# Four start-up memsets moved from GpSimd to VectorE, matmuls on ones ahead of the first transposes, and the order of 2,902 jobs read from a table

## The chip, the cores and the metric

The kernel runs on one core of one Trainium2 chip. A core has five engines with instruction streams of their own: TensorE (PE; PEld is its weight load), VectorE (DVE), ScalarE (ACT), GpSimd (POOL) and SyncE (SP). They meet through semaphores. SP and POOL issue the DMAs here, and sixteen DMA engines move the data. The metric is device time in microseconds.

## The reference

Linformer attention in 8 batches with 8 heads, 1024 tokens and head size 64, followed by a gated feed-forward layer on the 8192 tokens:

```python
k_proj = np.einsum('ks,bhsd->bhkd', E, k)            # 1024 keys become 64
v_proj = np.einsum('ks,bhsd->bhkd', F, v)
scores = scale * np.matmul(q, k_proj.transpose(0, 1, 3, 2))
scores = scores - np.max(scores, axis=-1, keepdims=True)
attn = np.exp(scores)
attn = attn / (np.sum(attn, axis=-1, keepdims=True) + 1e-09)
x = np.matmul(attn, v_proj)                          # as (8192, 512)
gate = 1.0 / (1.0 + np.exp(-(x @ w_gate)))           # w_gate, w_val: (512, 1536)
val = x @ w_val
out = gate * val @ w_out                             # w_out: (1536, 512)
```

Inputs and output are float32; the matmuls run in bfloat16.

## The kernel before

**Tiling.** A batch is cut into two blocks of 512 tokens. For each batch the kernel projects keys and values by E and F, transposes the queries (by DMA through SP from batch 1 on), computes scores, subtracts the row maximum, takes the exponential, multiplies by the projected values and transposes the quotient into `xT`. The gated layer of a block then reads `xT`. Most of its products are done as seven smaller products instead of eight (`seven`, `o_jobs`), so VectorE and GpSimd add and subtract operands and partial results; the first block and parts of the last go the plain way (`plain_steps`, `o_plain`). Eight PSUM banks (`pF0` to `pF3`, `pA0` to `pA3`) and thirteen float32 buffers of 512 columns hold what is in flight; two of the buffers lie in `EF`.

**The start.** `start_loads` issues E and F on SP (L629). On POOL it first sets the four 32-partition pieces of `quad` to 0, 32, 64 and 96 (L635) and then issues 25 loads (L569) in this order: keys, first query half and again for the other four heads, values, quarters of the gate and value weights, with the second query halves between them. `constants` builds identity matrices on VectorE: a row of counts by doubling (L660), its first 32 columns transposed (L667), `quad` added (L669), and comparisons into `identf`, `ident` and `minus` (L675, L682). It then clears `kpd` (L689) and two `vpD` (L693), and writes columns of ones (L696). `project_consts` turns E and F by eight float32 transposes on TensorE (L528) into two banks, and ACT copies both to `EFT` (L542).

**What sets the order.** Everything after that is a *job*: a Python function that issues one or more instructions on one engine, with a position given by the tables `AT` and `FB`. A `Scheduler` plays the program forward with costs, release times (`K_AT`, `Q_AT`, `V_AT`, `LAND`) and due positions. Whenever an engine of its model is free it takes the first job that is ready and for which a bank or buffer is free, so it decides the order on each engine and the place of each bank and buffer. When TensorE has nothing to do before its 25th microsecond it places a filler: two matmuls of 128 columns on `ident` into bank 7, which nobody reads. `Plan` adds the semaphore waits that follow from the resulting order, and each engine runs its list strictly in that order.

**Names in the trace.** Nearly all matmuls have L528, all ACT copies and functions L542, plain sums of two operands L557 on VectorE or GpSimd, loads L569. On VectorE L914 copies projected keys, L989 sums exponentials, L1645 takes the maximum, L1672 subtracts it, L886 copies out of PSUM, L1066 multiplies gate and value. Stores of a row block are L1312, of half a row block L1370, both on SP.

```python
            load_part(1, v, 0)
            for th in range(2):
                load_part(1, v, 1, th)
            load_w(0, 0)
            load_w(0, 1)
            load_w(3)
            load_w(1)
            for R in range(2):
                load_q_half(0, 1, R)
            load_w(4)
            load_w(2)
            load_w(5)
```

Of the kernel before, what the change touches and what calls it, by code (L numbers as in the profile page):

```python
# [12 lines left out]
P = 128  # L13
S = 1024
DH = 64
# [138 lines left out]
class Job:  # L154
    def __init__(self, eng, pos, body, release, name):
        self.eng, self.pos, self.body, self.release, self.name = eng, round(pos, 6), body, release, name
        self.cost, self.bytes, self.dma, self.port = 0.0, 0, False, False
        self.deps, self.slots, self.start, self.end = {}, [], None, None


class Scheduler:

    TAIL = {"PE": 0.0, "ACT": 0.115, "DVE": 0.09, "POOL": 0.15, "SP": 0.0}
    HOP = {"PE": 0.205, "ACT": 0.035, "DVE": 0.035, "POOL": 0.06, "SP": 0.1}

    EXTRA = dict(
        qt=0.12, qt1=0.16, turnk=0.1, turnk0=0.1, tp=0.1, tx=0.1, tk=0.1, tq=0.1, bc0=0.8, den0=0.2, xo0=0.2,
        copyG=0.028, copyV=0.028, copyO=0.028, tanh=0.015, kd=0.1, vd=0.1,
    )

    def __init__(self, banks, bufs, t0, window, landed, busy0, warm):
        self.jobs, self.now, self.t0, self.window, self.landed = [], None, t0, window, landed
        self.busy0, self.warm, self.fillers = busy0, warm, []
        self.writers, self.readers = {}, {}
        self.free = {
            "bank": {b: t0 for b in banks},
            "buf": {b: t0 for b in bufs},
        }
        self.clean = {b: False for b in banks}
        self.groups = []  # L180
        self.reads = []
        self.more = {"ACT": AT["pact"], "DVE": AT["pdve"], "POOL": AT["ppool"]}

    def job(self, eng, pos, body, release=0.0, name=""):
        j = Job(eng, pos, body, release, name)
        self.jobs.append(j)
        self.now = j
        body()
        j.cost += self.EXTRA.get(name, 0.0)
        self.now = None  # L190
        return j

    def note(self, eng, r, w, x, dma, cost, nbytes, port):
        j = self.now
        j.port = j.port or port
        assert eng == j.eng, (eng, j.eng, j.name)
        j.cost += cost
        j.bytes += nbytes
        j.dma = j.dma or dma is not None

        def dep(o, raw):
            if o is not j:
                j.deps[o] = j.deps.get(o, False) or raw

        for k in tuple(r) + tuple(w) + tuple(x):
            if isinstance(k, tuple) and isinstance(k[1], Slot) and k[1] not in j.slots:
                j.slots.append(k[1])
                k[1].left += 1
        for k in r:
            if k in self.writers:  # L210
                dep(self.writers[k], True)
        for k in tuple(w) + tuple(x):
            if k in self.writers:
                dep(self.writers[k], False)
            for o in self.readers.get(k, ()):
                dep(o, False)
        for k in r:
            self.readers.setdefault(k, []).append(j)
        for k in tuple(w) + tuple(x):
            self.writers[k] = j  # L220
            self.readers[k] = []

    def seen(self, o, eng, raw):
        if o.dma:
            return o.end + 0.1
        if o.eng == eng:
            if eng == "PE":
                return o.start + o.cost
            return o.end + 0.02
        if o.eng in ("ACT", "DVE", "POOL") and eng == "PE":  # L230
            return o.end + 0.055
        return o.end + self.HOP[o.eng]

    def safe(self, group, got):
        left = {k: len(f) for k, f in self.free.items()}
        left["clean"] = sum(self.clean[b] for b in self.free["bank"])
        for g, b in got:
            left[g.kind] -= 1
            if g.kind == "bank":
                left["clean"] -= self.clean[b]  # L240
        taken = [g for g, _ in got]
        todo = []
        for g in self.groups + ([] if any(group is x for x in self.groups) else [group]):
            need, held = dict.fromkeys(left, 0), dict.fromkeys(left, 0)
            for x in g:
                if x.at is None and not any(x is y for y in taken):
                    need[x.kind] += 1
                    need["clean"] += x.clean
                elif x.left:
                    held[x.kind] += 1  # L250
                    held["clean"] += x.kind == "bank" and not x.dirty
            todo.append((need, held))
        while todo:
            for i, (need, held) in enumerate(todo):
                if all(need[k] <= left[k] for k in left):
                    for k in left:
                        left[k] += held[k]
                    del todo[i]
                    break
            else:  # L260
                return False
        return True

    def take(self, j, t):
        got = []
        for s in j.slots:
            if s.at is not None:
                continue
            taken = [b for g, b in got if g.kind == s.kind]
            mine = [b for b, a in self.free[s.kind].items() if a <= t and b not in taken]  # L270
            if s.kind == "bank":
                if s.clean:
                    mine = [b for b in mine if self.clean[b]]
                elif s.dirty:
                    rough = sum(not c for c in self.clean.values()) + sum(self.clean[b] for _, b in got)
                    mine = [b for b in mine if not self.clean[b] or rough < (7 if t < 25.0 else 3)]
                mine.sort(key=lambda b: (self.clean[b], self.free["bank"][b]))
            else:
                mine.sort(key=lambda b: self.free["buf"][b])
            if not mine:  # L280
                return False
            got.append((s, mine[0]))
        if not got:
            return True
        group = got[0][0].group
        if not self.safe(group, got):
            return False
        if not any(group is g for g in self.groups):
            self.groups.append(group)
        for s, b in got:  # L290
            s.at = b
            del self.free[s.kind][b]
            if s.dirty:
                self.clean[b] = False
        return True

    def running(self, j):
        return any(x.group is g for x in j.slots for g in self.groups)

    def place(self, j, t):  # L300
        j.start = t
        j.cost *= 1 + self.more.get(j.eng, 0.0)
        if j.port:
            if j.eng == "DVE":
                j.cost += max(0.0, self.held - t)
                self.lock = t + j.cost
            if j.eng == "POOL":
                j.cost += max(0.0, self.lock - t)
                self.held = t + j.cost
        j.end = t + j.cost + self.TAIL[j.eng]  # L310
        if j.dma:
            begin = max(self.pipe, t + j.cost + 1.3)
            self.pipe = begin + j.bytes / 390e3
            j.end = self.pipe + 0.9 + AT["pdma"]
        self.busy[j.eng] = t + j.cost
        for s in j.slots:
            s.left -= 1
            s.end = max(s.end, j.end + (0.25 if j.eng == "PE" else 0.055))
            if s.left == 0:
                self.free[s.kind][s.at] = s.end  # L320
                if s.kind == "bank" and not s.clean:
                    self.clean[s.at] = not s.dirty
                if all(x.at is not None and not x.left for x in s.group):
                    self.groups = [g for g in self.groups if g is not s.group]
        for k in self.after.get(j, ()):
            self.count[k] -= 1
            if self.count[k] == 0:
                ready = max([self.seen(o, k.eng, raw) for o, raw in k.deps.items()] + [k.release, self.t0])
                self.open[k.eng].append((k.pos, self.rank[k], ready, k))

    def run(self):
        engines = ("PE", "ACT", "DVE", "POOL", "SP")
        self.busy = dict(self.busy0)
# [4 lines left out]
        for j in self.jobs:  # L338
            self.count[j] = len(j.deps)
            for o in j.deps:  # L340
                self.after.setdefault(o, []).append(j)
# [1573 lines left out]
```

## Time and profile before

| what | value |
|---|---|
| time, median of 3 runs | 518.52 us (518.36 to 518.65) |
| profiled execution | span 517.0 us; its time outside the span is not recorded, the median is 1.5 us above the span |
| chain of work that ended last | PE 93%, DVE 5%, DMA 1% |
| TensorE's first matmul | at 5.49 us, when F has landed |
| stores, issue to landing | 2.3 us (median of 63) |
| DMA engines, mean | 138 GB/s over the span |
| HBM | 60.29 MB read, 16.78 MB written |

One row of a view "instructions in order of time" has the start, the length, the engine, the line, the operation and the tile it writes and reads; equal neighbours are merged (x12), and the bracket gives the idle time before and what ended it. A matmul row's length contains the pipeline, so the distance between starts tells the pace. The granted clock in the views is 1.00 everywhere.

### The profile page before, as it was taken

How to read it: one execution, taken by the hardware profiler on the slowest of the kernel's cores; microseconds unless marked ns; L12 is line 12 of the kernel's file. 1: busy time of each engine (PE TensorE's matmuls, PEld its weight loads, DVE VectorE, ACT ScalarE, POOL GpSimd, SP SyncE). 2: the span in 40 equal slices, each digit the busy share in tenths (PEclk: the TensorE clock that was granted, in tenths of full speed). 3: DMA queues.
4: the chain of work that ended last, by engine and by line, in shares of the span. 5: the costliest groups of instructions: out<-in, count | busy, mean ns of one | idle time of the engine just before them, and what ended most of it. 6: DMA issues, size and time to landing. Idle time of an engine off the chain costs nothing.

```text
span 517.0 us, 12313 instructions
## 1 busy us (share of the span) xinstructions
PE 508.4 (98%) x4786; PEld 428.2 (83%) x4786; DVE 444.8 (86%) x843; ACT 375.4 (73%) x715; POOL 171.6 (33%) x200
## 2 busy tenths in 40 slices
PE   5999999999999999999999999999999999999997
PEld 4655867889988898888988889888998889888885
DVE  5879998898999799996999969997999969999570
ACT  1566966879977697777967689776877779677752
POOL 9882004802353024430344313630244303403200
DMA  9999928796689636994489926997369963610204
GB/s 160 198 198 207 202 64 161 117 215 136 123 174 203 161 58 129 187 185 132 82 160 170 191 76 95 188 204 146 77 113 183 202 143 62 145 42 1 82 1 164
DMA packets 140522, 71.59 MB, mean 138 GB/s; under 512 B 97200, under 2 KB 132272, under 8 KB 140464
## 3 DMA queue, kind: packets, MB, share of 16 engines
q0 software_dynamic: 35904, 29.89, 37.4%
q1 hardware_dynamic: 104560, 40.91, 36.9%
q8 instruction: 38, 0.62, 0.5%
q14 instruction: 20, 0.16, 0.1%
HBM read 60.29 MB, written 16.78 MB: 149 GB/s over the span
## 4 chain that ended last, share of the span: by engine, by line
PE 93%; DVE 5%; DMA 1%; ACT 0%; issue 0%; POOL 0%; SPq 0%
PE pA L528 47%; PE pF L528 46%; DVE topf L1645 1%; DVE hT L1066 1%; DMA EF<-in_F_dram 1%; DVE pA L1672 1%; DVE pF L1672 1%; DVE inv L989 0%; ACT KVs L542 0%; POOL wT L996 0%; DVE tG L557 0%; ACT ost L542 0%; DVE inv L990 0%; DVE eT L886 0%; DVE xT L886 0%
## 5 line engine op out<-in xcount | busy, mean ns | idle before, releaser
L542 ACT ACTIVATE spare<-pF 128x512 f32<-128x512 f32 (+2 forms) x167 | 93.7, 572 | 30.5 <-PE pF L528 27.6
L557 POOL TENSOR_TENSOR hT<-hT,hS 128x512 bf16<-128x512 bf16 x42 | 48.6, 1184 | 193.7 <-PE pA L528 155.1
L542 ACT ACTIVATE spare<-pA 128x512 f32<-128x512 f32 (+2 forms) x150 | 85.1, 582 | 15.6 <-PE pA L528 12.0
L542 ACT ACTIVATE spare<-spare 128x512 f32<-128x512 f32 x77 | 48.5, 635 | 25.7 <-DVE spare L1156 25.4
L1734 POOL TENSOR_TENSOR KVs<-spare,inv 128x384 bf16<-128x384 f32 (+1 forms) x50 | 36.6, 738 | 86.9 <-ACT spare L542 43.6
L528 PE MATMUL pA<-wO,hT 128*128 128x256 bf16 (+1 forms) x408 | 60.7, 288 | 0.0
L1225 DVE SCALAR_TENSOR_TENSOR hT<-spare,pF 128x512 bf16<-128x512 f32 x73 | 48.9, 679 | 7.6 <-ACT spare L542 3.6
L528 PEld LDWEIGHTS pA<-wO,hT 128*128 128x128 bf16 x408 | 39.9, 98 | 10.4
L1156 DVE TENSOR_TENSOR spare<-pF,spare 128x512 f32<-128x512 f32 x62 | 41.8, 681 | 3.7 <-PE pF L528 2.0
L528 PE MATMUL pF<-xT,wV 128*128 128x256 bf16 (+1 forms) x276 | 44.7, 283 | 0.0
L528 PE MATMUL pF<-xS,tV 128*128 128x256 bf16 x248 | 37.3, 273 | 0.0
L1156 DVE TENSOR_TENSOR spare<-pA,spare 128x512 f32<-128x512 f32 x53 | 35.7, 676 | 1.3 <-ACT spare L542 0.8
L528 PE MATMUL pA<-xT,wG 128*128 128x256 bf16 (+1 forms) x212 | 34.1, 283 | 0.0
L528 PE MATMUL pF<-xS,wV 128*128 128x256 bf16 x224 | 33.6, 272 | 0.2 <-ACT KVs L542 0.2
L1225 DVE SCALAR_TENSOR_TENSOR hT<-spare,pA 128x512 bf16<-128x512 f32 x41 | 27.7, 679 | 5.8 <-PE pA L528 3.8
L528 PE MATMUL pF<-xT,wG 128*128 128x256 bf16 (+1 forms) x196 | 32.4, 288 | 0.2 <-DVE xT L886 0.2
L528 PEld LDWEIGHTS pF<-xT,wV 128*128 128x128 bf16 x276 | 26.6, 98 | 5.9 <-issue 0.2
L528 PE MATMUL pA<-wT,hT 128*128 128x256 bf16 x240 | 31.1, 272 | 0.0
L1672 DVE TENSOR_TENSOR pF<-pF,topf 128x512 f32<-128x512 f32 x45 | 29.7, 689 | 0.0
L1645 DVE TENSOR_REDUCE topf<-pF 128x8 f32<-128x512 f32 x45 | 29.3, 678 | 0.0
L528 PE MATMUL pF<-wO,hT 128*128 128x256 bf16 (+1 forms) x204 | 29.3, 285 | 0.0
L528 PE MATMUL pA<-wT,hS 128*128 128x256 bf16 x216 | 29.1, 273 | 0.0
(183 smaller groups left out, 1267.0 us busy)
## 6 DMA issues: line engine op xcount, KB each, us to landing
out_dram<-ost SPq DMA_DIRECT2D x63, 256.0 KB, 2.3
KVs<-in_v_dram POOLq DMA_DIRECT2D x15, 512.0 KB, 11.2
KVs<-in_k_dram POOLq DMA_DIRECT2D x14, 512.0 KB, 7.6
Qb<-in_q_dram POOLq DMA_DIRECT2D x14, 512.0 KB, 15.7
wO<-in_moe_w_out_dram POOLq DMA_DIRECT2D x1, 1536.0 KB, 28.5
wG<-in_moe_w_gate_dram POOLq DMA_DIRECT2D x5, 256.0 KB, 16.8
wV<-in_moe_w_val_dram POOLq DMA_DIRECT2D x5, 256.0 KB, 17.5
KVs<-in_k_dram POOLq DMA_DIRECT2D x4, 256.0 KB, 6.8
```

The lines of the kernel that those rows point to most:

```text
L528: lambda e: e.matmul(o, lhsT, rhs, **kw),
L542: lambda e: e.activation(o, i, func, scale=scale),
L557: fn = lambda e: e.tensor_tensor(o, a, b, op)
L1066: lambda e: e.scalar_tensor_tensor(hT[0][:, m, :], BF(sg), 1.0, PB(bv)[:, :], ALU.add, ALU.mult),
L1156: lambda e: e.tensor_tensor(PB(b)[:, :] if stay else BF(s), PB(b)[:, :], BF(s), ALU.add),
L1225: lambda e: e.scalar_tensor_tensor(o, y.rearrange("p (j c) -> p j c", j=2), 1.0, x.rearrange("p (j c) -> p j c", j=2), ALU.add, ALU.mult,),
L1645: lambda e: e.tensor_reduce((top if by_pe(b, t, y) else topf)[:, n : n + 8], PB(bk)[:, :].rearrange("p (n k) -> p n k", n=8), mybir.AxisLi ...
L1672: lambda e: e.tensor_tensor(x, x, topf[:, n : n + 8].unsqueeze(2).to_broadcast([P, 8, 64]), ALU.subtract),
L1734: fn = lambda e: e.tensor_tensor(xto.rearrange("p (g h d) -> p h g d", g=2, h=H)[:, hh[0] : hh[1], :, :], o[:, :, 0:DH].rearrange("p (h g) ...
```

## The change

- The four memsets of `quad` move from POOL, where they stood ahead of the first load, to VectorE, behind the transposition of the counts.
- VectorE first sets a new tile `warm` (128 x 128, bfloat16) to one. Ten matmuls of 512 columns on it, into bank 7, stand on TensorE ahead of the transposes of E and F.
- Of the two copies to `EFT`, ACT does the first and VectorE the second.
- The two memsets of `vpD` are written as float32, 520 columns instead of 1040.
- A filler is one matmul of 256 columns instead of two of 128. There are 35 of them instead of 45 pairs (90).
- The `Scheduler` keeps no costs any more. A table `ORDER` gives the order of all jobs (-1 is a filler), a table `PLACES` the bank or buffer of each. The 2,902 jobs, their engines and what they compute are those of before. Of the jobs on TensorE 868 of 1,054 stand at another place in its list, by up to 30 places; on VectorE 646 of 814, by up to 32; on ACT 524 of 712, POOL 109 of 167 and SP 94 of 155.

In POOL's list a load of keys of batch 1 comes ahead of eight sums of weights and of the two query loads of batch 1; before it stood behind them. In SP's list the last stores come in another order: the store of the last block's first row block stands behind that of the first half row block, and the last one is the same. On TensorE the matmuls after the last filler are the same, in another order.

The two tables, cut to their first lines, and the rest of the diff without the removed scheduler:

```diff
+ORDER = (
+    0, -1, -1, -1, 1, 2, 3, -1, -1, -1, -1, -1, -1, 12, 4, 13, 14, 5, -1, -1, 6, 15, 16, 22, 17, -1, -1, 7, 23,
...
+    def run(self, fill):
+        groups = []
         for j in self.jobs:
...
+            self.now = j
+            j.body()
+            for s in j.slots:
+                if not any(s.group is g for g in groups[-40:]):
+                    groups.append(s.group)
+        self.now = None
+        slots = [s for g in groups for s in g]
+        assert len(ORDER) - ORDER.count(-1) == len(self.jobs) and len(PLACES) == len(slots)
+        for s, p in zip(slots, PLACES):
+            s.at = p
+        return [fill if i < 0 else self.jobs[i].body for i in ORDER]
...
-            for i in range(4):
-                pool(
-                    lambda e, i=i: e.memset(quad[32 * i : 32 * i + 32, :], 32.0 * i),
-                    w=[("quad", i)],
                 )
...
         def constants():
+            dve(lambda e: e.memset(warm[:, :], 1.0), [], ["warm"])
             dve(lambda e: e.memset(count[:, 0:1], 0.0), [], ["count"])
...
             dve(lambda e: e.transpose(rows[:, :], pats[:, :]), ["pats"], ["rows"])
+            for i in range(4):
+                dve(lambda e, i=i: e.memset(quad[32 * i : 32 * i + 32, :], 32.0 * i), [], [("quad", i)], n=1)
...
-                dve(lambda e, i=i: e.memset(vpD[i][:, :, :, :], 0.0), [], vk, n=520)
+                dve(
+                    lambda e, i=i: e.memset(
+                        vpF[i][:, :].bitcast(FP32), 0.0
+                    ),
...
+        def warm_up():
+            for _ in range(10):
+                mm(7, bank[7][:, :], warm[:, :], warm[:, :].unsqueeze(1).to_broadcast([P, 4, P]), ["warm"])
...
-                act(
-                    EFT[:, 4 * g : 4 * g + 4, :].rearrange("p t c -> p (t c)"),
-                    bank[b][:, :],
-                    [],
-                    [("EFT", g)],
-                    b=b,
-                )
-
-        def busy(n):
-            for _ in range(n):
-                mm(7, bank[7][:, 0:P], ident[:, :], ident[:, :], ["ident"], n=P)
+                o = EFT[:, 4 * g : 4 * g + 4, :].rearrange("p t c -> p (t c)")
+                if g:
+                    dve(lambda e, o=o, b=b: e.tensor_copy(o, bank[b][:, :]), [], [("EFT", g)], b=b)
+                else:
+                    act(o, bank[b][:, :], [], [("EFT", g)], b=b)
+
+        def busy():
+            mm(7, bank[7][:, 0 : 2 * P], ident[:, :], ident[:, :].unsqueeze(1).to_broadcast([P, 2, P]), ["ident"], n=2 * P)
...
         start_loads()
         constants()
+        warm_up()
         project_consts()
```

More of the change, by code (lines that the diff above doesn't have):

```diff
@@ L154, with __init__, note @@
 class Job:
[L155 to L158, printed above, removed]
-class Scheduler:
[L163 to L168, printed above, removed]
-    )
[L171 to L182, printed above, removed]
-    def job(self, eng, pos, body, release=0.0, name=""):
[L185 to L193, printed above, removed]
-        j = self.now
[L195 to L203, printed above, removed]
+    def __init__(self, eng, body, name):
+        self.eng, self.body, self.name, self.slots = eng, body, name, []
+ORDER = (
[154 rows of a table added]
+)
+PLACES = (
[27 rows of a table added]
+)
+class Scheduler:
+    def __init__(self):
+        self.jobs, self.now = [], None
+    def job(self, eng, pos, body, release=0.0, name=""):
+        self.jobs.append(Job(eng, body, name))
+    def note(self, eng, r, w, x):
+        j = self.now
+        assert eng == j.eng
         for k in tuple(r) + tuple(w) + tuple(x):
@@ L207, in note @@
                 j.slots.append(k[1])
[L208 to L329, printed above, removed]
@@ L331, in run @@
-    def run(self):
-        engines = ("PE", "ACT", "DVE", "POOL", "SP")
-        self.busy = dict(self.busy0)
-        self.pipe, self.held, self.lock = self.landed, 0.0, 0.0
-        self.rank = {j: i for i, j in enumerate(self.jobs)}
-        self.after, self.count = {}, {}
-        self.open = {e: [] for e in engines}
-        for j in self.jobs:
-            self.count[j] = len(j.deps)
-            for o in j.deps:
-                self.after.setdefault(o, []).append(j)
-            if not j.deps:
-                self.open[j.eng].append((j.pos, self.rank[j], max(j.release, self.t0), j))
-        import heapq
-        todo = [(j.pos, self.rank[j], j) for j in self.jobs if j.eng == "PE"]
-        heapq.heapify(todo)
-        left, t = len(self.jobs), self.t0
-        while left:
-            moved = True
-            while moved:
-                moved = False
-                while todo and todo[0][2].start is not None:
-                    heapq.heappop(todo)
-                limit = (todo[0][0] if todo else 1e9) + self.window
-                for e in engines:
-                    if self.busy[e] > t + 1e-9:
-                        continue
-                    best = None
-                    for item in sorted(self.open[e], key=lambda i: (i[0], i[1])):
-                        if item[0] > limit and not self.running(item[3]):
-                            continue
-                        if item[2] <= t + 1e-9 and self.take(item[3], t):
-                            best = item
-                            break
-                    if best is not None:
-                        self.open[e].remove(best)
-                        self.place(best[3], t)
-                        left -= 1
-                        moved = True
-                    elif e == "PE" and t < self.warm and self.fillers:
-                        j = self.fillers.pop()
-                        self.jobs.append(j)
-                        self.rank[j] = len(self.jobs)
-                        self.place(j, t)
-                        moved = True
-            after = [b for b in self.busy.values() if b > t + 1e-9]
-            after += [i[2] for e in engines for i in self.open[e] if i[2] > t + 1e-9]
-            after += [a for f in self.free.values() for a in f.values() if a > t + 1e-9]
-            if left:
-                assert after, [(e, i[0], i[3].name) for e in engines for i in sorted(self.open[e])[:6]]
-                t = min(after)
-        return sorted(self.jobs, key=lambda j: (j.start, self.rank[j]))
@@ L479, in bass_linformer_attn__then__ffn_glu_sigmoid_kernel @@
         plan = Plan()
-        busy0 = {"PE": 7.35, "ACT": 8.2, "DVE": 7.7, "POOL": 19.7, "SP": 7.35}
-        sched = Scheduler(range(8), range(2 + NB), 7.35, AT["window"], 37.0, busy0, 25.0)
-        sched.free["bank"][7] = 25.2
+        sched = Scheduler()
         def add(eng, fn, r=(), w=(), x=(), dma=None, cost=0.0, nbytes=0, port=False):
             if sched.now is not None:
-                sched.note(eng, r, w, x, dma, cost, nbytes, port)
+                sched.note(eng, r, w, x)
                 return None
@@ L873, in first_batch @@
                         job(eng, p, lambda R=R, g=g, hf=hf, b=bb[g], eng=eng: h_xo_keep(hf, R, g, b, eng), name="xok")
-            for _ in range(170):
-                j = Job("PE", 9e9, lambda: busy(2), 0.0, "fill")
-                sched.now = j
-                busy(2)
-                sched.now = None
-                j.deps = {}
-                sched.fillers.append(j)
         def copy(eng, o, i, r, w, b, n):
@@ L1882, in bass_linformer_attn__then__ffn_glu_sigmoid_kernel @@
             plan.readers[("buf", i)] = [o for n in "EF" for o in plan.readers[("EF", n)]]
-        for j in sched.run():
-            j.body()
+        for body in sched.run(busy):
+            body()
         plan.emit(nc, es, final=[f"out{i}" for i in range(4)])
```

18 lines of the change are left out of this document (11 added, 7 removed), and 180 rows, old and new, of tables (ORDER, PLACES).

## The prediction, as it was put on record

> **What bounds the kernel now.** I read the page first, then busy time in stretches of 13 us, then who waited for whom, then the instructions in order of time over the start.
>
> ```profile
> span 517.0 us, 12313 instructions
> ...
> PE 508.4 (98%) x4786; PEld 428.2 (83%) x4786; DVE 444.8 (86%) x843; ACT 375.4 (73%) x715; POOL 171.6 (33%) x200
> ```
>
> TensorE is busy for all but 8.6 us of the span. A modelled busy time can hide slow stretches, so the matmuls themselves must be counted (columns: stretch, length, then busy time and instructions of PE, PEld, DVE, ACT, POOL, then granted clock, DMA share, GB/s):
>
> ```profile
> 0.00:13.00 13.00, 7.51 (x74) 5.90 (x74) 7.54 (x26) 2.48 (x3) 12.24 (x24) 1.00 1.09 160
> 13.00:26.00 13.00, 12.92 (x176) 9.09 (x172) 10.85 (x23) 7.09 (x14) 11.33 (x16) 1.00 1.41 198
> ...
> 39.00:52.00 13.00, 12.77 (x112) 7.84 (x110) 12.93 (x33) 8.40 (x17) 2.46 (x3) 1.00 1.24 207
> 208.00:221.00 13.00, 13.00 (x121) 11.52 (x119) 12.76 (x23) 10.65 (x21) 4.91 (x7) 1.00 1.00 181
> ```
>
> In the last row 121 matmuls, nearly all of 256 columns, take 13.00 us: 107.4 ns each. A 256-column product can hardly go faster: a 128-column one takes 56 ns in the unbroken row at 10.75 below. So from about 26 us on TensorE runs without holes, and a new order can only lose there. The waits of TensorE in the whole run say the same:
>
> ```profile
> PE pF L528 <- DMA EF<-in_F_dram: 5.5, 1, 5.5
> PE pF L528 <- DVE xT L886: 0.2, 1, 0.2
> PE pF L528 <- ACT KVs L542: 0.2, 1, 0.2
> ```
>
> So there is something to win in three places only: the first 26 us, two short waits (at 49.2 and 80.3 us), and the tail behind the last matmul. The start, in order of time (start, duration):
>
> ```profile
> 0.75 0.56 POOL L635 MEMSET quad<- 32x1 f32 x4 [0.29 <-POOLq L1900]
> ...
> 1.37 1.68 POOL L569 DMA_DIRECT2D KVs<-in_k_dram  x2
> ...
> 5.49 1.94 PE L528 MATMUL pF<-tV,EF 128*128 128x128 f32 x8 [5.49 <-DMA EF<-in_F_dram]
> ...
> 6.62 0.60 ACT L542 ACTIVATE EFT<-pF 128x512 bf16<-128x512 f32 x1 [4.59 <-PE pF L528]
> ...
> 7.47 0.60 ACT L542 ACTIVATE EFT<-pF 128x512 bf16<-128x512 f32 x1 [0.26 <-PE pF L528]
> ...
> 8.36 1.46 PE L528 MATMUL pA<-ident 128*128 128x128 bf16 x12
> ...
> 9.75 1.06 PE L528 MATMUL pF<-KVs,EFT 128*64 128x256 bf16 x8
> ...
> 10.75 0.86 PE L528 MATMUL pA<-ident 128*128 128x128 bf16 x12
> 10.88 0.88 DVE L914 TENSOR_SCALAR kpd<-pF 64x256 bf16<-64x256 f32 x2 [3.23 <-PE pF L528]
> ```
>
> The rows pA<-ident are filling matmuls that no one reads; there are 90, the last two at 25.91. The twelve at 8.36 are issued 107 ns apart, those at 10.75 56 ns apart: the TensorE clock doubles 5.3 us after the first matmul, though the granted clock reads 1.00 throughout. The twelve slow ones end at 9.64, while the second quarter of the keys, issued at 2.30, has landed by 8.5 (6.2 later): its projection at 9.75 is over 1 us late for nothing.
>
> **The change part by part.**
>
> *Fillers.* 90 of 128 columns (12 x 107 + 78 x 56 ns = 5.65 us) become 35 of 256 (35 x 107 ns = 3.75 us): 1.9 us less of the stream of TensorE, if the work that they waited for comes sooner.
>
> *Ten matmuls on ones ahead.* 512 columns at the slow rate are 4 x 107 = 427 ns, ten are 4.3 us. They start when VectorE's first memset is done (some 0.15 us behind its first instruction at 0.82) and end near 5.3, in TensorE's idle time before F lands (5.40). The clock should then be open near 5.5 instead of 10.8: eight transposes at 107 instead of 213 ns, two projections of keys with 0.43 instead of 0.85 us each. If they ran over F's landing, each would cost 0.43.
>
> *The second EFT copy goes to VectorE.* ACT's two copies end at 8.07; side by side both end before 8.0. VectorE is free for it: its next work is the row at 10.88, behind 3.23 of idle time.
>
> *VectorE's constants.* One memset of 128 columns and four of one column more, about 0.1 each: the chain to the identity grows by 0.5 (3.84 to about 4.3), still ahead of F at 5.40; without that cover it costs 0.5. The two memsets of vpD halve their elements: 0.93 to about 0.49 (the row of kpd, 512 words, 0.48). Nothing waits for them.
>
> *The chain at the start.* Second key projection at about 8.2 instead of 9.75 (key landing 8.5 less the shift below, behind three fillers): 1.55; 0.43 for its duration. From the key copies (10.88 to 8.9) on, the chain scores, maximum, exponential, sum, norm, transposes is the same instructions in nearly the same order, so it reaches the second attention product (24.69) 2.0 us sooner, at 22.7. The query and key landings (9.84 to 13.86, each about 0.5 sooner) just do not hold it back.
>
> *The loads.* The first key load is issued 0.62 sooner, all of the queue behind it too (POOL issues every 0.74, a piece takes 1.33 to transfer: the engines are the limit). But until 4.1 the sixteen engines move E and F (share 0.99 from 3.0 to 4.5). Between 0 and 0.62 I take 0.5, as engines with key packets show shares of 1.46 and so have room for both. F may land 0.3 later for it; the 0.75 us that TensorE has to spare (next) hide that.
>
> *What is late next: the weights.* In the new order TensorE's first product on the third quarter of the gate weights has the same work ahead of it as before, where it starts at 35.65. That piece is issued at 16.80 and lands 18.1 later, at 34.9:
>
> ```profile
> wG<-in_moe_w_gate_dram POOLq DMA_DIRECT2D x1, 256.0 KB, 18.1
> ...
> 35.65 0.59 PE L528 MATMUL pF<-xT,wG 128*128 128x512 bf16 x2
> ```
>
> So TensorE can be early by 0.75 plus the shift of 0.5 and not by 2.0: **1.25 us**. (The last query piece, 30.8 against 31.72, leaves 0.9 plus 0.5.)
>
> *Order and banks further on.* The two waits, 0.23 at 49.20 (a cast on VectorE) and 0.16 at 80.34, have other products ahead of them in the new order: 0.35 gained; bounds 0 and 0.4. VectorE is packed from 31.9 to 61.3 (28.45 of 29.40), but starts that stretch sooner with TensorE. The key load of batch 1 goes past eight POOL sums and the two query loads in POOL's queue; the queries land some 2.5 later for it (one 512 KB piece), at 61.4 instead of 59.1 less the shift; four transposes of 1.3 on SP's queue follow, and the first score product that needs them is at 69.5: about 2 us of cover. New waits: below nothing is excluded, since TensorE has no holes; above, two waits of 0.16 in each of seven cycles are 2.2. Counting in both orders how much TensorE work stands between a result and the product that needs it, less the duration of the copy between, ten places are short in the new order and nine in the old, by at most 0.15; I take 0.2 lost.
>
> *Tail.* The last half row block stays last (ACT 0.38 at 514.39, its store, the end). In SP's queue one 256 KB store now stands just ahead of that last store: 0 to 0.4, taken as 0.1 lost.
>
> Sum: -1.25 - 0.35 + 0.2 + 0.1 = -1.3. Span 517.0 to 515.7. The median of the runs is 518.52, 1.5 over the span, and that stays: **517.2 us**.
>
> **The rivals.** *(1) The key loads do not come sooner.* The first key packet moves at 4.1, 2.7 us behind its issue; in the DMA view up to 4.1 only q1 (E and F) has packets. At 210.03, with that queue empty too, it takes 1.5. VectorE's chain of constants ends at 4.2. If the loads wait for that chain, they start 0.35 to 0.5 later than now, and the gain at the weights is 0.75 - 0.4 = 0.35: 518.1. Against it: the issues themselves go on at 0.75 us each beside that chain. The Trainium skill (SBUF — State Buffer, section "SBUF: two separate sides") names such a cause: a VectorE operation in a two-port mode locks out GpSimd, which then cannot write the descriptors of its DMAs. By that rule the four memsets moved to VectorE would not free the loads but delay them; the 2.7 against 1.5 us agree, no run so far shows the cause.
>
> *(2) Slower: the fixed order waits in the dense cycles.* Place: products that follow an ACT copy of their own bank (0.57 us, L542) by one 0.43 us product. Price: 0.16 to 0.4 a time. With one such wait of 0.35 in each of the seven cycles the loss is 2.5, against 1.5 won: 519.5. It decides from 0.2 per cycle (no gain) and 0.37 (slower by over 0.2%). For it: VectorE's 12.93 of 13 at 39 to 52. Against it: the count of short places is the same as before.
>
> *(3) The whole 2.0 comes through*, if the loads gain more than their issue does (the shorter memsets lie where DMA falls from 196 to 156 GB/s, 6.0 to 7.5): -2.0 - 0.35 + 0.1 = 516.2.
>
> **How the numbers follow.** Forecast 0.52, (3) 0.10, (1) 0.18, (2) 0.20. The measurement tells 0.2%, 1.04 us, from no change: below 517.5 is faster, above 519.6 slower. The forecast with its bounds (shift 0 to 0.62, waits, tail) runs from 516.8 to 518.3, some 0.1 of it above 517.5. Faster: 0.44 + 0.10 and 0.04 of (1) and (2), 0.58. Slower: 0.12 of (2). Same: 0.30. The range from 516.1 to 519.0 leaves out the worse part of (2) and little else.
>
> **What would show it.** Right: first key issue near 0.8 and packets near 3.5; matmuls on ident 107 ns apart for 256 columns from the first; the second attention product near 22.7; a short wait of TensorE for a weight or query landing between 28 and 36; no wait for ACT or DVE beyond 0.2 later. Wrong: key landings not earlier (1), PE waits on L542 or L557 past 40 us (2), slow transposes at 5.5.

## The result: 1.2% slower, and the profile after

| | before | after |
|---|---|---|
| median of 4 runs each, same chip | 518.59 us (518.36 to 519.34) | 525.10 us (523.46 to 525.81) |
| ratio after / before, 95% interval | | 1.0119 (1.0102 to 1.0136) |
| span of the profiled execution | 517.0 us | 521.7 us |

The forecast was 517.2 us. The profile is of the fastest of the four runs, 523.46 us; why the others are longer is explained below. The head of its page:

```profile
span 521.7 us, 12142 instructions
...
PE 510.9 (98%) x4737; PEld 426.1 (82%) x4741; DVE 446.4 (86%) x849; ACT 374.5 (72%) x714; POOL 171.3 (33%) x196
```

TensorE is busy for 98% as before; what is left of the span is 10.8 us against 8.6, and 4.3 us of its busy time are the new matmuls on ones. **The start** went nearly as planned. In order of time, the rows that answer to those of before:

```profile
1.06 4.33 PE L519 MATMUL pA<-warm 128*128 128x512 bf16 x10 [1.06 <-DVE tV L643]
...
1.27 1.67 POOL L560 DMA_DIRECT2D KVs<-in_k_dram  x2 [0.82 <-POOLq L1891]
...
5.79 1.13 PE L519 MATMUL pF<-tV,EF 128*128 128x128 f32 x8 [0.39 <-issue]
...
7.11 0.69 DVE L717 CAST EFT<-pF 128x512 bf16<-128x512 f32 x1
...
8.24 0.63 PE L519 MATMUL pF<-KVs,EFT 128*64 128x256 bf16 x8
...
8.94 0.88 DVE L905 TENSOR_SCALAR kpd<-pF 64x256 bf16<-64x256 f32 x2 [1.14 <-PE pF L519]
```

The ten matmuls on ones run at 427 ns each until 5.39, the transposes of F start at the fast clock, and the second key projection stands at 8.24 instead of 9.75. One part did not come: the first key load starts at 1.27, only 0.10 sooner than the 1.37 of before, though nothing stands ahead of it. Then busy time in the same stretches as before:

```profile
0.00:13.00 13.00, 11.19 (x87) 6.25 (x88) 9.10 (x35) 1.92 (x3) 11.94 (x20) 1.00 1.11 168
...
39.00:52.00 13.00, 12.89 (x118) 8.26 (x116) 12.89 (x32) 9.51 (x20) 2.83 (x3) 1.00 1.24 207
208.00:221.00 13.00, 11.99 (x110) 10.26 (x108) 12.53 (x21) 7.93 (x16) 5.66 (x7) 1.00 1.03 178
```

From 208 to 221 us TensorE, full before with 121 matmuls, has 110 and a hole of 1.0 us. Followed along the same work, the changed kernel is 1.3 us ahead at 30.6, 1.5 ahead from 125 to 200, and 4.7 behind from 342 to the end. So 6.2 us are lost, net, all between 200 and 342. Who waited, for the whole run (columns: who and what, releaser, us in total, times, longest):

```profile
PE pF L519 <- DVE hT L1216: 2.9, 2, 2.2
PE pF L519 <- issue: 1.2, 2, 0.8
...
PE pA L519 <- ACT pA L533: 1.0, 1, 1.0
PE pA L519 <- DVE hS L548: 0.4, 1, 0.4
```

The losses are at six places: 1.2 at 213, 0.6 at 257 to 262 (landings of two transposes), 2.4 at 287, 0.9 at 296 (a key load, below), 0.6 and 0.9 at 338 and 340. They are counted from one matmul's start to the next, less the usual distance, and so each is some 0.17 longer than in the view of the waits; they add up to 6.6, of which 0.4 is won back between them. At the first and the largest, in the timelines of GpSimd, VectorE and TensorE:

```profile
210.54 0.75 POOL L560 DMA_DIRECT2D KVs<-in_k_dram  x1
210.80 2.23 DVE L548 TENSOR_TENSOR hT<-hT 128x1024 bf16<-128x1024 bf16 x1
211.29 1.18 POOL L548 TENSOR_TENSOR xS<-xT,xS 128x512 bf16<-128x512 bf16 x1
...
284.76 0.79 POOL L560 DMA_DIRECT2D KVs<-in_k_dram  x1
284.98 3.41 DVE L1216 SCALAR_TENSOR_TENSOR hT<-spare 128x512 bf16<-128x512 f32 x1
285.56 2.27 POOL L548 TENSOR_TENSOR hT<-hT,hS 128x512 bf16<-128x512 bf16 x2
...
289.85 0.61 PE L519 MATMUL pF<-xS,wV 128*128 128x256 bf16 x4 [2.23 <-DVE hT L1216]
```

An operation of VectorE that takes 0.68 us elsewhere takes 3.41 here. It starts in a load issue of GpSimd, lies through two GpSimd sums and ends 0.56 behind them, as if it had done nothing before they ended. At 210.80 another takes 2.23 instead of 0.68, at 336.89 one takes 2.13 instead of 0.42; both start in a load issue with a GpSimd sum behind it, and both last until that sum has ended. **Theory:** VectorE stands still while GpSimd reads its operands, and the tables put such sums right behind load issues and beside results that TensorE wants next. The Scheduler of before kept an account of this (`held`, `lock`); the tables replaced it. In the traces two of GpSimd's 124 sums stand right behind a load issue before, and six after. Before, VectorE was held up too: against the same operations in the runs without GpSimd's sums (experiment 2), 15 were longer, by 12.1 us in sum, and after 11, by 11.1. But before none took more than 1.37 (0.95 above its normal duration), all were `xS` sums, and none of them is among TensorE's waits. **Rivals:** the edits of the start do the harm; the order waits for results whoever computes them; GpSimd's load issues, not its sums, hold VectorE.

### The profile page after: what moved, and what is told of

The parts are those of the page before. It is cut to its first block, busy times and chain, and to the rows that moved or that the text cites. A ratio compares the mean times of both kernels' runs of the same rounds, so it can differ in the third digit from the quotient of the medians.

```text
span 521.7 us, 12142 instructions
## 1 busy us (share of the span) xinstructions
PE 510.9 (98%) x4737; PEld 426.1 (82%) x4741; DVE 446.4 (86%) x849; ACT 374.5 (72%) x714; POOL 171.3 (33%) x196
## 4 chain that ended last, share of the span: by engine, by line
PE 93%; DVE 3%; ACT 1%; issue 1%; DMA 1%; DVEq 0%
PE pA L519 47%; PE pF L519 46%; DVE hT L1216 1%; DMA eT<-KVs 1%; DVE pF L1147 0%; DVE hT L1057 0%; DVE hS L548 0%; ACT spare L533 0%; ACT ost L533 0%; ACT vpD L533 0%; DVE wT L987 0%; DVE inv L980 0%; DVE ost L1405 0%; DVE EF L1147 0%; ACT EF L533 0%
## 5 line engine op out<-in xcount | busy, mean ns | idle before, releaser
L1725 POOL TENSOR_TENSOR KVs<-spare,inv 128x384 bf16<-128x384 f32 (+1 forms) x45 | 32.9, 739 | 91.0 <-DVE spare L1147 40.8
L519 PE MATMUL pA<-wO,hT 128*128 128x256 bf16 (+1 forms) x358 | 51.3, 286 | 0.1
L519 PEld LDWEIGHTS pA<-wO,hT 128*128 128x128 bf16 x360 | 34.9, 98 | 8.7
L519 PE MATMUL pF<-xT,wV 128*128 128x256 bf16 (+1 forms) x248 | 39.0, 281 | 0.0
L519 PE MATMUL pF<-wO,hT 128*128 128x256 bf16 (+1 forms) x250 | 36.5, 287 | 0.1
L519 PE MATMUL pA<-xS,tG 128*128 128x256 bf16 x208 | 30.7, 273 | 0.0
L519 PE MATMUL pA<-xS,wG 128*128 128x256 bf16 x200 | 29.8, 272 | 0.0
L519 PEld LDWEIGHTS pF<-wO,hT 128*128 128x128 bf16 x252 | 24.5, 98 | 6.1
L519 PE MATMUL pF<-xT,wG 128*128 128x256 bf16 (+1 forms) x176 | 28.5, 285 | 0.0
L519 PE MATMUL pA<-xT,wV 128*128 128x256 bf16 (+1 forms) x160 | 27.2, 291 | 1.0 <-ACT pA L533 1.0
```

The source lines that it names most:

```text
L519: lambda e: e.matmul(o, lhsT, rhs, **kw),
L1725: fn = lambda e: e.tensor_tensor(xto.rearrange("p (g h d) -> p h g d", g=2, h=H)[:, hh[0] : hh[1], :, :], o[:, :, 0:DH].rearrange("p (h g) ...
```

## Experiments

Each time is beside runs of the kernel before on the same chip; the ratio sets these two beside each other. The runs without GpSimd's sums leave that part of the computation out.

| run | median us | before | ratio (95%) |
|---|---|---|---|
| start edits, old order | 518.18 | 518.81 | 0.9989 (0.9980 to 0.9998) |
| tables, old start | 525.04 | 518.81 | 1.0110 (1.0091 to 1.0129) |
| after without GpSimd's sums | 517.99 | 518.81 | 0.9985 (0.9976 to 0.9995) |
| before without GpSimd's sums | 519.17 | 518.81 | 1.0002 (0.9993 to 1.0011) |
| after, four sums on VectorE | 525.44 | 518.88 | 1.0127 (1.0090 to 1.0165) |
| after, three entries moved | 519.32 | 518.88 | 1.0008 (0.9995 to 1.0020) |
| start edits, planned anew | 519.16 | 518.88 | 1.0010 (1.0000 to 1.0019) |
| load moved alone | 521.22 | 519.16 | 1.0045 (1.0030 to 1.0060) |
| two sums moved alone | 522.73 | 519.16 | 1.0073 (1.0055 to 1.0092) |
| three moved, old start | 519.62 | 519.16 | 1.0013 (1.0001 to 1.0026) |
| three moved, quad on GpSimd | 519.14 | 519.16 | 1.0004 (0.9993 to 1.0014) |

**1. Start or order?** The edits of the start in the kernel before, and the tables with the old start.

> The kernel before with all edits of the start (four memsets of quad on VectorE, ten matmuls on ones, second copy of EFT on VectorE, memsets of vpD by 32-bit words) and its old order, written by the Scheduler with unchanged release times and 90 small fillers. Theory (the start gains, the order of the tables loses it again): 517.2 us, 1.3 under before; the projections at 8.2 and the second attention product about 1.5 sooner, and no wait of TensorE over 0.4 us after 60 us. Rival (the edits of the start themselves cost time, through the loads): 519 or more.

> The changed kernel with the old start (quad on GpSimd, both copies of EFT on ScalarE, old memsets of vpD, no matmuls on ones), so only order, banks and fillers are those of the tables. Theory (the order alone carries the loss): 525 to 527 us, with waits of TensorE of over 0.5 us beyond 200 us. Rival (start edits and order only lose together, because the start shifted what the order met): at most 520.

518.18 and 525.04: the order alone carries the whole loss. With the old start VectorE's operations beside the same GpSimd sums take 1.84, 3.41 and 2.14 us; at the first place it is the operation behind the one that was held in after. The longest:

```profile
286.43 3.41 DVE L1206 SCALAR_TENSOR_TENSOR hT<-spare 128x512 bf16<-128x512 f32 x1
```

TensorE loses 1.0, 2.4, 0.6 and 0.9 behind them. The start edits alone gain 0.1% and not 1.3 us: TensorE waits 0.5 for values at 16.8, the second attention product is 0.9 sooner and not 1.5, and then it waits for queries (0.22 at 31.65).

**2. GpSimd's reading?** The sums become memsets of the same output.

```diff
-                pool(fn, r, w, cost=n / 485 + 0.06, port=True)
+                pool(lambda e: e.memset(o, 0.0), r, w, cost=n / 485 + 0.06, port=True)
```

> The changed kernel with GpSimd's two-operand sums replaced by memsets of the same output, which read nothing; the sums are left out of the computation. Theory (VectorE's operations with two operands in SBUF stand still while GpSimd reads SBUF for a sum, and TensorE waits for what they produce): the operations of 2.2 to 3.4 us on VectorE at 211, 285 and 337 us take 0.7 to 1.3, some 5 us of waits go, 519 us; a wait of 0.9 for the keys and values near 296 stays. Rival (the order waits for results whoever computes them, or GpSimd's load issues are what holds VectorE): the long operations stay, 523 or more.

> The kernel before with the same sums replaced by memsets, in the order that it has with them. Theory (here the standstill falls where nobody waits): within 0.7 us of before, 518 to 519, though VectorE's operations with two operands lose their long cases. Rival (leaving the sums out shortens any order, so that the gain of the changed kernel without them says nothing about its loss): 515 or less.

517.99 and 519.17. Without the sums the changed kernel is 7.1 us shorter than its first measurement, the kernel before no shorter at all. The operation that took 3.41 is in the timeline of this run

```profile
284.05 0.68 DVE L1216 SCALAR_TENSOR_TENSOR hT<-spare 128x512 bf16<-128x512 f32 x1
```

so it is not the order as such that waits. The time was better than expected: the wait at 296 went too, since the load behind the shorter memsets is issued at 282.5 and lands at 292.7, before TensorE wants it. In this condition the change is 1.2 us under the kernel before. That is only about what it would be worth without the hold, because a memset is also shorter than a sum (0.53 against 1.15 us in experiment 4), so GpSimd gets to its loads sooner.

**3. Which sums?** First, four of them (one at 211, two at 285, one at 337) go to VectorE in place.

```diff
+FOUR = (1036, 1648, 1646, 1772)
...
+            if SWAP[0]:
+                eng = "DVE"
```

> The changed kernel with four of GpSimd's sums on VectorE instead, in the same place of the written order: those that run beside the long operations at 211, 285 (two) and 337 us. Theory (VectorE stands still for exactly these sums): operations of over 2 us go at the three places, with them about 4.5 us of TensorE's waits; 519.5 to 521. Rival (any sum on GpSimd in this order costs, or VectorE has no room for four more): the waits only move, 523 or more.

The expectation failed: 525.44. The long operations are gone from all three places, and yet:

```profile
PE pF L532 <- issue: 3.5, 1, 3.5
...
KVs<-in_k_dram POOLq DMA_DIRECT2D x1, 512.0 KB, 12.6
```

This wait, from 293.0 to 296.5, is for half of the keys. Their load stands behind two other GpSimd sums, the first of which waits 6.5 us for TensorE; it is issued at 283.85 and lands 12.6 later, at 296.43. In after it was issued at 284.76 and landed at 297.04, and TensorE, late through the first delay, came at 296.36 and waited only 0.78 for it. So there are **two** delays at 283 to 297, and they lie beside each other: taking one away shows the other. Followed along the same work, this run is 3.3 ahead of after at 290; it loses 2.7 of that at the keys, 1.6 behind them at half the clock (experiment 6) and 1.0 at 430, where a transpose lands late. Second, the three entries of the table that stand wrong are moved, nothing else:

```diff
 # in ORDER, GpSimd's queue
-1022, 1018, 1036 ... 1755, 1758, 1772 ... 1647, 1538, 1386, 1648, 1646
+1036, 1022, 1018 ... 1772, 1755, 1758 ... 1386, 1647, 1538, 1648, 1646
```

(1036 and 1772 are sums for `xS`, 1386 is the key load, 1647, 1648 and 1646 are `hT` sums; the rest are loads and one more sum for `xS`.)

> The changed kernel with three entries of the order table moved, all on GpSimd's queue: the sums for xS at 211 and 337 us ahead of the loads that they stood behind, and the key load at 284.8 ahead of the sums that it stood between. Nothing is left out. Theory (a sum right behind load issues locks VectorE from the issue on, a sum behind other work only for its own 1.15 us): no operation of VectorE over 1.7 us at the three places, 518 to 520. Rival (the loads are innocent; sums lock VectorE wherever they stand): the long operations stay or move with the sums, 522 or more.

519.32, no different from before: three places in 2,902 made the loss. The two moved `xS` sums now run at 206.76 and 327.52, well ahead of the loads. The four sums from 281 on are still back to back, and VectorE now gets its turn after one; TensorE's wait for it falls from 2.2 to 0.3:

```profile
283.69 1.48 DVE L1185 SCALAR_TENSOR_TENSOR hT<-spare 128x512 bf16<-128x512 f32 x1
...
286.64 0.61 PE L488 MATMUL pF<-xS,wV 128*128 128x256 bf16 x4 [0.30 <-DVE hT L1185]
```

The three other sums right behind a load issue, at 24.64, 95.03 and 415.01 in after, stay where they are; none of VectorE's operations beside them is long in after's trace. The moves one by one:

> The changed kernel with one of the three moves of the reordered version: the key load at 284.8 us goes ahead of the sums that it stood between. Theory (three sums behind one another take turns with VectorE, and the load lands before TensorE wants it at 293): the wait of 2.4 at 287 falls to some 0.5, the 0.9 at 296 goes, those at 213 and 340 stay at 1.2 and 1.4; 520.5 to 522, granted clock 1.00 in all runs. Rival (the two sums for xS carry most of the loss): 523 or more.

> The changed kernel with the other two moves: the sums for xS at 211 and 337 us go ahead of the loads. Theory: the waits at 213 and 340 go (1.2 and 1.4), the 2.4 at 287 and the key load's late landing at 296 to 297 stay; since that landing does not come sooner than TensorE, 522 to 524, and some runs show a granted clock under 1.00. Rival (without those two waits TensorE meets the rest with slack): under 521.

521.22 and 522.73: both times are within their expectations, but not every part of them came. In the first run nothing waited at 337, though the sum stood where it was. There VectorE's last operation with two SBUF operands ended at 335.70, and the sum behind the load issues (336.85 to 338.03) met only operations with an operand in PSUM. So the collision is a matter of phase. Instead TensorE waited 0.9 for keys at 356, which was not expected, so it is in part luck that the time fits. In the second run the key load landed at 295.23, 1.8 sooner than in after though issued no sooner, and TensorE did not wait for it.

**4. The hold by itself.**

> No attention and no layer is computed, only this: ten equal operations of VectorE of 512 columns back to back (two bf16 operands in SBUF; two float32 operands in SBUF; one operand in PSUM; one operand only), beside nothing, one or three sums on GpSimd, one or three load issues, load issues followed by a sum, and memsets on GpSimd. Theory: sums hold up VectorE's operations with two operands in SBUF by 1.1 us each, load issues alone and memsets by under 0.1, a sum behind load issues by the issue's 0.75 more; operations with an operand in PSUM or with one operand run on. Rival (load issues hold VectorE too): over 0.3 us beside the issues alone.

Duration of the slowest operation of VectorE, in us, by what GpSimd does beside it, from the profile of one execution:

| VectorE's operation | nothing | 1 sum | 3 sums | 3 load issues | issue, sum | 2 issues, sum | issue, 2 sums |
|---|---|---|---|---|---|---|---|
| two bf16 operands in SBUF | 0.42 | 1.38 | 1.37 three times | 0.42 | 1.76 | 2.21 | 2.90 |
| two float32 operands in SBUF | 0.69 | 1.64 | 1.63 three times | 0.69 | 1.83 | 2.61 | 2.97 |
| one operand in PSUM | 0.68 | | 0.68 | | | 0.68 | |
| one bf16 operand, copy | 0.29 | | 1.24 three times | | | 2.07 | |

Three memsets on GpSimd instead of sums change nothing (0.42, 0.69). Load issues hold nobody by themselves. But a sum queued behind one holds VectorE already during that issue, and two sums behind an issue run through with no turn for VectorE. With a sum, an issue and a sum, two operations are held, 1.37 and 2.00 (bf16). One part of the expectation failed: the copy, with one operand, does not run on but is held too. Timelines of the cases "issue, sum", "2 issues, sum", "issue, 2 sums" and of one operand in PSUM beside three sums:

```profile
42.16 0.75 POOL L159 DMA_DIRECT2D Q<-in_q_dram  x1 [0.30 <-POOL poolf L168]
42.61 1.76 DVE L138 TENSOR_TENSOR outd<-ina,inb 128x512 bf16<-128x512 bf16 x1
42.92 1.17 POOL L150 TENSOR_TENSOR poolout<-poola,poolb 128x512 bf16<-128x512 bf16 x1
...
49.95 2.21 DVE L138 TENSOR_TENSOR outd<-ina,inb 128x512 bf16<-128x512 bf16 x1
50.70 1.17 POOL L150 TENSOR_TENSOR poolout<-poola,poolb 128x512 bf16<-128x512 bf16 x1
...
59.02 2.90 DVE L138 TENSOR_TENSOR outd<-ina,inb 128x512 bf16<-128x512 bf16 x1
59.37 2.26 POOL L150 TENSOR_TENSOR poolout<-poola,poolb 128x512 bf16<-128x512 bf16 x2
...
192.21 0.68 DVE L144 TENSOR_TENSOR outd<-ps,fina 128x512 bf16<-128x512 f32 x1
```

At 42.61 VectorE's operation starts 0.31 us before the sum's row does, at 49.95 it starts 0.75 before, time enough to finish its 0.42. Both still end 0.29 behind the sum, as an operation beside a single sum does: VectorE is held before the sum's row begins. This pattern is that of the 2.23 at 210.80 and of the 3.41 at 284.98. The Trainium skill (SBUF — State Buffer, section "Who interferes with whom") says that a VectorE instruction with two inputs in SBUF contends with a GpSimd instruction that reads SBUF, that a fast copy does too, and that whoever issues first has the port for the whole instruction. The traces agree: 1.38 against 0.42 beside a sum, 1.24 against 0.29 for the copy, 0.68 in both cases for the operand in PSUM, nothing beside a memset. Who issued first the traces do not show; by the start of the rows VectorE was first at 49.95, and it was VectorE that waited.

**5. What the start is worth, and a better plan.**

> The reordered version (all three moves) with the old start: quad on GpSimd, both copies of EFT on ScalarE, old memsets of vpD, no matmuls on ones. It shows what the edits of the start are worth when the order has no long waits. Theory (the start gains 1.3 to 2.0, held back only by the weights' landing): 1.2 to 2.0 over the reordered version of the earlier call, 520.5 to 521.3. Rival (the start's gain is given back at later landings of keys and queries): within 0.6 of it.

> The reordered version with the four memsets of quad back on GpSimd ahead of the first key load, all else of the new start kept. Theory (the first load starts only 0.1 us sooner without them, its first packet no sooner): within 0.4 of the reordered version, key landings within 0.4. Rival (what the change's first part is for: the loads come 0.6 sooner): 0.5 or more over it.

> The edits of the start with the Scheduler of before, which knows GpSimd's hold on VectorE, told when the new start has its data: release times of the new loads, engines free 0.35 to 1.05 sooner. No tables. Theory (start gain and an order planned with the hold): 516.5 to 517.5, under the kernel before and under the start edits with the old order (518.2). Rival (the third quarter of the weights lands no sooner than TensorE's first use, so nothing more is to be had): 518 to 518.5.

519.62, 519.14 and 519.16. With the three entries moved, the profiles show the same work 1.25 us sooner with the new start than with the old from 146 to 204 us, as forecast. Yet each median is about as far above the kernel before on its own chip (519.32 by 0.44, 519.62 by 0.46): the rival holds. The later waits are for landings, and they differ between runs:

```profile
PE pA L486 <- DMA KVs<-in_v_dram: 0.9, 1, 0.9
PE pF L486 <- DMA KVs<-in_k_dram: 0.5, 1, 0.5
```

in the run with the old start; 1.4 for a key transpose at 425 us in the one with quad on GpSimd. The ten runs of the version with three moved entries lie between 517.99 and 520.68; that landings make this spread is likely from these rows, but only one of its runs has a trace, so it is not shown. With quad back on GpSimd nothing is lost: the first load starts at 1.38 instead of 1.27, its first packet moves at 4.18, against 3.87 to 4.30 in the eight profiles with the new start. The new plan missed its expectation: it has waits for keys and values (0.4 and 0.6) that the kernel before does not have, and 0.2 more at 265 us. In its edit ScalarE is told to be free 1.05 sooner and TensorE 0.7, but GpSimd only 0.1 sooner and VectorE 0.15 later. Of all versions that compute the whole, the start edits with the old order are the fastest, by 0.1%: less than the 0.2% that counted as a difference in the forecast.

**6. The rest of the time: the clock.** Two of the four runs of after have a mean granted clock of 0.997; they took 525.44 and 525.81 us, the two at 1.000 took 523.46 and 524.75. The tables with the old start have a profile of such a run. Stretches of TensorE's row around the wait at 288.9, then behind it:

```profile
288.47:291.30 2.83, 0.60 (x6) 0.29 (x4) 2.73 (x4) 0.72 (x2) 0.81 (x1) 1.00 1.33 164
291.30:294.70 3.40, 3.40 (x17) 2.40 (x18) 1.22 (x3) 1.19 (x2) 0.00 (x0) 0.52 1.60 75
```

and the same work in after's profile:

```profile
289.85:293.25 3.40, 3.40 (x32) 3.05 (x33) 1.97 (x4) 2.03 (x4) 0.00 (x0) 1.00 1.37 141
```

17 matmuls against 32 in 3.4 us: after a wait of the same 2.2 us, one run is granted half the clock for 3.41 us and loses 1.6 there, the other is not. Part of it is not lost for good: the run at half the clock comes to the keys at 299.40, when they have landed (297.59), while after's profile waits 0.78 for them. The two runs of after at 0.997 are 1.5 longer in the mean than the two at 1.000, but these differ by 1.3 between themselves, so what the clock costs a whole run is known only roughly. All four runs of "two sums moved alone", which keep that wait, show 0.997; all of "load moved alone", without it, 1.000; "four sums on VectorE", with a wait of 3.5, 0.993 to 0.997. The Trainium skill (TensorE: Matmul & The Clock Gate, section "Part 1: The HAM clock gate") has the clock fall after at least one idle window of about 3.4 us that runs freely. Half the clock lasted 3.41 us here, as one such window; but 2.2 us of waiting were enough to bring it about.

## Why the prediction was wrong, point by point

- **The step that failed: "New waits ... I take 0.2 lost", with bounds 0 and 2.2.** It measured 6.2 in the profile, and more where the clock fell. I had counted TensorE's work between a result and its use against the result's *nominal* duration. What the runs show in its place: three VectorE operations held for 2.1 to 3.4 us by GpSimd sums right behind load issues, and a key load queued behind sums; moving three entries takes the loss from 6.5 us over before to 0.4. I did not ask what the tables do with such durations. The bound 2.2 (two waits of 0.16 a cycle) is from TensorE's own rows; the row that bounds it is VectorE's longest operation. The code had a model of it, and the trace of before showed that durations are not nominal: the `xS` sums take 1.23 and 1.29 instead of 0.42 in six cycles, beside three GpSimd sums:

```profile
162.28 3.56 POOL L557 TENSOR_TENSOR hT<-hT,hS 128x512 bf16<-128x512 bf16 x3 [9.18 <-PE pA L528]
162.48 1.23 DVE L557 TENSOR_TENSOR xS<-xT 128x512 bf16<-128x512 bf16 x1
...
164.83 1.29 DVE L557 TENSOR_TENSOR xS<-xS,xT 128x512 bf16<-128x512 bf16 x1
```

- **Rival (2)** ended on the right side, but its mechanism was wrong (a bank waiting for its ACT copy; the one late wait that names ACT, at 213, is for an ACT copy that waited for VectorE, where the operation that it needed stood behind the held one), and so was its price, 2.5.
- **Start: right.** Matmuls on ones until 5.39 (forecast 5.3), fast transposes, copies done at 7.80 (before 8.0), second key projection 8.24 (8.2), key copies 8.94 (8.9), second attention product 23.03 (22.7). Fillers 35 instead of 90, as worked out.
- **"The loads: ... I take 0.5": wrong.** The first issue moved by 0.10, not 0.62: GpSimd's own preparation, 0.82 us idle ahead of the issue, seems to have gone on behind the memsets. In after's profile the weights landed 0.65 sooner, but over eight profiles with the new start and four with the old one the third quarter of the gate weights lands at 34.6 and 34.7 in the mean, between 34.1 and 35.1. Rival (1) had the loads no sooner, and they were not; nor were they later, as it had it: the first packet moves at 3.87 to 4.30 with the four memsets on VectorE (eight profiles) and at 3.87 to 4.18 with them on GpSimd (five). Its cause is not borne out either: in experiment 4, beside VectorE's packed stream of copies, a load's first packet moved 1.5 us after its issue, no later than elsewhere in that run (1.45 to 1.82).
- **"TensorE can be early by ... 1.25": right in size** (1.33 at 30.6, 1.25 in the pair of profiles of experiment 5), though the shift of 0.5 in it was chance. That it stays to the end was not right: the medians of experiment 5 show nothing of it, and the later waits that the profiles show are for landings.
- **"The two waits ... 0.35 gained": 0.21.** Counted from matmul to matmul, 0.27 and 0.24 us remain at 47.8 and 79.4, where 0.40 and 0.32 stood. **Tail** 0.1 lost: 0.02 (from the last matmul's end to the span's end 2.66 against 2.64).
- **"1.5 over the span": too little.** In the 65 later executions of the kernel before with both numbers on record the time is 1.74 to 1.95 over the span, 1.83 in the mean. So the profile of before is of an execution of some 518.8, by estimate, and the sum's 515.7 would have meant 517.5. Beside the loss this is small.

## What to carry to other kernels

A fixed order is as good as the model that it is made with: if an operation's duration depends on what another engine does beside it, the order must be planned or searched with that, and on the chip. Give GpSimd's sums with SBUF operands a place where no VectorE result with two SBUF operands is due, never right behind a load issue, and do not queue a load behind sums that wait. When a stall has gone and the time has not, look for the second delay that lay beside it.

## What the runs showed of the hardware

- A GpSimd sum queued behind two load issues held VectorE for 0.75 us before its own row started, behind one for 0.31; two sums behind an issue give VectorE no turn (2.90 us for an operation of 0.42), while three sums with no issue ahead alternate strictly with VectorE (1.37 each).
- After a wait of TensorE of 2.2 us the granted clock is half for 3.41 us in some runs of the same kernel (1.6 us lost in that stretch) and full in others; why it falls in one and not in another no run shows.
- How a full queue of loads lands differs by up to 1 us between runs (third quarter of the gate weights 34.1 to 35.1), more than the 0.5 by which the change at the start was to bring them forward.
